# Top-k attention and two MLPs on one core: first value loads issued after key transposes, half of the second weights' low parts on GpSimd, later value norms at later steps

## The chip, the cores and the metric

One NeuronCore of a Trainium2 chip runs the whole program in one launch. The metric is the device time of an execution in microseconds. The kernel before took 1135.48 us (median of three runs, 1133.12 to 1138.31); the execution whose profile is shown here took 1133.29 us, of which the first to the last instruction span 1131.5 us. The engines are called as the profile calls them: PE (TensorE matmul) and PEld (its weight loads), DVE (VectorE), ACT (ScalarE), POOL (GpSimd), SP (SyncE, which only issues DMAs here). A queue of an engine runs in the order in which the program lists it: an instruction that waits holds everything behind it.

## The reference

Attention over 4 batches, 8 heads, 576 positions and head size 64, in which each row keeps only its 32 largest scores; then two MLPs on the 2304 tokens of width 512, with 2048 hidden units each.

```python
scores = (1/8) * q @ k.T                       # 4 x 8 x 576 x 576
kth = the 32nd largest of each row
attn = softmax(where(scores >= kth, scores, -1e9))
x = (attn @ v), heads side by side              # 2304 x 512
h = x @ w_in1;  g = where(h >= 1, h, where(h <= -1, 0, (h+1)**2/4));  y = g @ w_out1
out = relu(y @ w_in2)**2 @ w_out2
```

All inputs and the output are float32, and the result keeps float32-like accuracy by splitting each operand into a float16 high part and a float16 low part and adding three products.

## The kernel before

**Work.** The attention runs as 144 slots, one head of one tile of 128 query rows each (18 tiles T, 8 heads). A slot is: scores on PE into the PSUM tile `both`, which has room for two slots; eight DVE passes (four `max` for eight values each, `match_replace` between them) that find the 32nd largest score; `below` and `exp` on ACT into the tile `W`, for which POOL makes the bias `nb`; high part `pc` on ACT, low part on POOL; a DMA transpose of both parts (`pT`) on SP; the product with the values on PE (`acc`). After a tile's eight slots the tokens go through MLP 1 and then MLP 2, in 144 groups of 512 hidden units: in products (`h`), activation (`r`), split (`g`), a DMA transpose (`gT`), out products (`o`).

**Weights.** Four matrices of 16 chunks of 128x512 each (`i1`, `o1`, `i2`, `o2`) are loaded, decoded into a form of their own by ACT, POOL and DVE (`w_decode`, L475), squared into a Gram matrix on PE for a power-of-two scale (`w_norm`, L493), and split into high and low half (`w_split`, L519), where the two halves of a chunk overwrite the place of the chunk before it. For `i1` and `o1` the split is: high = scaled copy on ACT; low = two PE products into PSUM (a diagonal of the scale times the float32 chunk, less the high part: `lo_i`, `lo_o`), copied out by ACT. For `i2` and `o2`: scale in place (even chunks on ACT, odd ones on POOL), high = copy on ACT, low = subtraction on POOL.

**Values.** `v_load_early` (L619) brings the first batch's values in three DMAs of 512, 128 and 640 KB. For the batches 1 to 3, 24 pieces of the values are loaded and squared once more ahead of time for their scales (`norm_load`, `norm`, tile `n_v`); then `kv_scale`, `meet_consts`, `mlp1_consts` and `mlp2_consts` make scales and constants in small DVE instructions.

**Order.** Every instruction is recorded by `note` (L183) with the step u at which the table PLAN (L35) puts it; a slot has eight steps, so slot s begins at step 8s, and MLP group n stands 12 slots behind its slot number. `order` (L271) then lists the instructions of each engine: it plays the program with assumed costs (`costs`, L247), and of what is ready it takes the lowest step. The real program waits only on data; what `order` decides is each queue's sequence. Every instruction is emitted by one helper line, so all rows carry L348 (L356 after the change) and are told apart by their tiles. In the names, the number of a tile's buffer follows the name (`pT_339`), and rows of the profile leave it out; the program's weights, first keys and first values all live in one tile, `wall`.

The steps that the change touches: `v0l` is the step of `v_load_early`; `vn`, `vnd` and `vnl` set the first step, spacing and load lead of the 24 norms; `vs`, `meet`, `mc1` and `m2c1` the steps of the scales and constants.

Of the kernel before, what the change touches and what calls it, by code (L numbers as in the profile page):

```python
# [7 lines left out]
F16 = mybir.dt.float16  # L8
# [4 lines left out]
AF = mybir.ActivationFunctionType  # L13
# [24 lines left out]
    d0=(-8, -6, -4, -2), l0=(-9, -6), n0=(0, 1, 0, 1, 2, 3), q01=-5, v0l=-2, v0n=(5, 7, 9, 11), v0s=14, vn=60, vnd=7,  # L38
    vnl=18, vs=241, meet=248, mc1=252, m2c0=121, m2c1=265, v0=(21, 25, 29, 33, 37, 41, 45, 49), kv1=(254, 10, 289, 6),
# [10 lines left out]
    g_gate=13, g_split=15, scores=-6, below=8, wbufs=4, md=(), exp=9, bias=7, phi=10, plo=11, ptr=13, att=30, acopy=29, li1d=3, lo1=0, lo1d=0, dsd_i1=(), dsd_o1=(), dsd_i2=(), dsd_o2=(), xu0=2,  # L50
    dk=(0, 1, 2), dv=(8, 11, 5, 7), dq=(), dsh_i1=(), dsh_o1=(), dsh_i2=(), dsh_o2=(), odd=0, klead=10, vlead=5, sbufs=3,
    vbufs=8, dsa_i1=(0, 2, 4, 6, 8, 10, 12, 14), dsa_o1=(0, 2, 4, 6, 8, 10, 12, 14),
    dsa_i2=(0, 2, 4, 6, 8, 10, 12, 14), dsa_o2=(0, 2, 4, 6, 8, 10, 12, 14), u0=-6,
# [93 lines left out]
class Book:  # L147
# [3 lines left out]
    def __init__(self, nc):  # L151
        self.ops, self.rings, self.step, self.beat = [], {}, 0, []
        self.paper = _bacc_().Bacc("TRN2", target_bir_lowering=False, num_devices=1)
        self.names = 0
        self.shift = 0

# [26 lines left out]
    def note(self, engine, method, fn, args, kwargs):  # L183
# [7 lines left out]
        deps = set()  # L191
# [11 lines left out]
        for v in ins:  # L203
            c = v.cover()
            deps.update(n for d, n in v.tile.writes if meet(c, d))
            v.tile.reads.append((c, op.n))
# [40 lines left out]
    def costs(self, engine, method, args, kwargs, outs, ins):  # L247
        n = outs[0].elements() if outs else 0
        if engine == "PE":
            a = args[1].tile.dtype  # L250
            c = max(n * (4 if a is F32 else 1) / 2370.0, 0.03)
            return c, c + 0.2
        both = sum(not v.tile.ring.psum for v in ins if v.elements() > 64)
        if engine == "DVE":
            if method in ("max", "match_replace"):
                n = 576
            c = 0.06 + n / 960 + (0.07 if method == "match_replace" else 0.25 if both > 1 else 0.06 if method != "max" else 0)
            return c, c + 0.03
        if engine == "ACT":
# [101 lines left out]
def tile_topk_attention_mlp_mlp(  # L361
# [155 lines left out]
    DIAG_AT = {"i1": (38, 38), "o1": (48, 56)}  # L517

    def w_split(name, c):  # L519
# [3 lines left out]
        if name in DIAG_AT:  # L523

            diag = wall[:, DIAG_AT[name][c // 8], 0:P]
            ps = []

            def high():
                if c == 0 or c == 8 and len(set(DIAG_AT[name])) == 2:
                    DVE.tensor_scalar(diag, ident, s, None, op0=ALU.mult)  # L530
                ACT.activation(hi, src, AF.Copy, scale=s)

            def low():
                ps.append(ps_h.tile([P, 4, P], F32, tag="h", name=f"lo_{name}_{c}").rearrange("p a b -> p (a b)"))
                PE.matmul(ps[0], diag, src, start=True, stop=False)
                PE.matmul(ps[0], neg, hi, start=False, stop=True)

            return [high, low, lambda: ACT.activation(lo, ps[0], AF.Copy)]
        on_dve, one = c in PLAN["dsd_" + name], c in PLAN["dsh_" + name]
        if on_dve:  # L540
            scale = lambda: None
            low = lambda: DVE.scalar_tensor_tensor(lo, src, s, hi, op0=ALU.mult, op1=ALU.subtract)
            if one:
                high = lambda: DVE.tensor_scalar(hi, src, s, None, op0=ALU.mult)
            else:
                high = lambda: ACT.activation(hi, src, AF.Copy, scale=s)
        else:
            if c in PLAN["dsa_" + name]:
                scale = lambda: ACT.activation(src, src, AF.Copy, scale=s)
            else:  # L550
                scale = lambda: POOL.tensor_scalar(src, src, s, 1.0, op0=ALU.mult, op1=ALU.mult)
            low = lambda: POOL.tensor_tensor(lo, src, hi, op=ALU.subtract)
            if one:
                high = lambda: POOL.tensor_scalar(hi, src, 1.0, 1.0, op0=ALU.mult, op1=ALU.mult)
            else:
                high = lambda: ACT.activation(hi, src, AF.Copy)
        return [scale, high, low]
# [70 lines left out]
    kst, vst, ld = {}, {}, {}  # L628

    def k_prep(b, i):  # L630
# [26 lines left out]
        def trans():  # L657
            ks = pool.tile([P, 9, P], F16, tag="kst", name=f"kst_{b}_{i}", bufs=4)
            SP.dma_start_transpose(out=ks, in_=hl().rearrange("p c a d -> p (c a d)"))
            for h in range(2):  # L660
                kst[b, 2 * i + h] = ks[:, :, 64 * h : 64 * h + 64]
# [96 lines left out]
    def q_prep(T, half):  # L758
# [21 lines left out]
        def trans():  # L780
            qt = pool.tile([P, 2, 4, P], F16, tag="qT", name=f"qT_{T}_{half}", bufs=2)
            SP.dma_start_transpose(
# [69 lines left out]
    def prob_hi(t):  # L852
# [3 lines left out]
        ACT.activation(d["hi"], d["e"], AF.Copy)  # L856
# [38 lines left out]
    def token_trans(src, dst, key, tag, name):  # L895
# [9 lines left out]
        def trans():  # L905
            tt = pool.tile([P, 2, 4, P], F16, tag=tag, name=f"T_{name}", bufs=1)
# [101 lines left out]
    NGROUP = 8 * NTILE + 4  # L1008
# [21 lines left out]
    def mlp_act(n):  # L1030
# [8 lines left out]
        else:  # L1039
            ACT.activation(r, h, AF.Relu, scale=C2)  # L1040
            ACT.activation(r, r, AF.Square)
# [9 lines left out]
    def mlp_split(n):  # L1051
# [3 lines left out]
        ACT.activation(g[:, 0], r, AF.Copy)  # L1055
# [200 lines left out]
    order = [(1, 0, j) for j in range(4)] + ([(2, 0, j) for j in range(4)] if PLAN["early"] else [None] * 4)  # L1256
    order += [(1, 1, j) for j in range(4)] + ([None] * 4 if PLAN["early"] else [(2, 0, j) for j in range(4)])
    for T in range(2, NTILE):
        order += [(1, T, j) for j in range(4)] + [(2, T - 1, j) for j in range(4)]
    order += [(2, NTILE - 1, j) for j in range(4)]  # L1260
# [96 lines left out]
```

## Time and profile before

| what | value |
|---|---|
| median of three runs | 1135.48 us |
| the profiled execution | 1133.29 us, span 1131.5 us |
| busy: PE, DVE, ACT, POOL | 991.0, 917.4, 865.9, 702.0 us |
| slots start: 0, 4, 12, 16, 20 | 26.4, 50.9, 121.8, 157.4, 203.3 us |
| slots start: 36, 140 | 321.0, 997.8 us |

The slots' starts are those of their first `max` on DVE in the trace. From slot 36 to slot 140 a slot takes 6.5 us on average; the first twenty take 8.8 us each, while the weights are loaded, decoded and split beside the attention. DVE has little left after slot 143; PE then works off the last groups of the MLPs.

### The profile page before, as it was taken

Reading aid. Unit: us, or ns where it says so; the run is one execution under the profiler, and the core shown is the slowest. Engines: PE = TensorE matmul, PEld = TensorE weight load, DVE = VectorE, ACT = ScalarE, POOL = GpSimd, SP = SyncE. Lnnn points to the kernel's source line nnn. Section 1 sums busy time; section 2 is a strip of 40 time slices with the busy share of each in tenths; the row PEclk is TensorE's granted clock in tenths of the full one; section 3 lists DMA queues with packets and bytes.
Section 4 is the critical chain, followed back from the end, with each engine's and each line's share of the span. In section 5 each row is a group of like instructions: output and inputs, shape, how many; then the busy total and the mean of one; then the engine's idle time right before and its main releaser. Section 6 shows DMA issues by size and latency. Waiting matters only on the chain. (4 is left out here: it accounts for less than half of the span.)

```text
span 1131.5 us, 20715 instructions
## 1 busy us (share of the span) xinstructions
PE 991.0 (88%) x6700; PEld 483.0 (43%) x6700; DVE 917.4 (81%) x1967; ACT 865.9 (77%) x1613; POOL 702.0 (62%) x1166
## 2 busy tenths in 40 slices
PE   2257795778899989999999999999999999999997
PEld 1134342334344444444444444444544544444443
DVE  4899977897989898999989899998899999982100
ACT  4678999899777687878888777888777788776532
POOL 4696759879676755557776746567774647453221
PEclk9969898899999999999999999999999999999999
DMA  9988868575798666868977676778868665555332
GB/s 261 336 252 238 242 151 197 132 152 104 150 161 149 110 119 110 158 116 160 165 149 142 118 121 127 150 138 159 151 126 136 118 130 110 112 107 98 70 61 56
DMA packets 463389, 165.22 MB, mean 146 GB/s; under 512 B 441776, under 2 KB 448944, under 8 KB 463280
## 3 DMA queue, kind: packets, MB, share of 16 engines
q1 hardware_dynamic: 463280, 163.90, 71.0%
q8 instruction: 52, 0.85, 0.3%
q14 instruction: 57, 0.47, 0.1%
HBM read 55.31 MB, written 4.72 MB: 53 GB/s over the span
## 5 line engine op out<-in xcount | busy, mean ns | idle before, releaser
L348 PE MATMUL o<-wall,gT 128*128 128x512 f16 x1728 | 418.9, 381 | 17.5 <-DMA gT<-g 17.1
L348 DVE MAX8 m<-W 128x8 f32<-128x576 f32 x432 | 326.9, 758 | 8.5
L348 POOL TENSOR_TENSOR pc<-W,pc 128x64 f16<-128x64 f32 (+1 forms) x288 | 209.1, 747 | 87.8 <-ACT pc L348 73.2
L348 POOL TENSOR_TENSOR g<-r,g 128x512 f16<-128x512 f32 x144 | 167.7, 1164 | 152.4 <-ACT g L348 127.8
L348 PEld LDWEIGHTS <-gT 128*128 128x128 f16 x1728 | 163.7, 98 | 219.2 <-DMA gT<-g 31.6
L348 PE MATMUL h<-wall,T_x 128*128 128x512 f16 x864 | 209.4, 384 | 10.1 <-DVE r L348 8.3
L348 DVE MATCH_REPLACE8 W<-m,W 128x576 f32<-128x576 f32 x288 | 213.8, 743 | 0.0
L348 PE MATMUL h<-wall,T_y 128*128 128x512 f16 x864 | 207.9, 379 | 2.7 <-ACT r L348 1.7
L348 ACT ACTIVATE W<-both,nb 128x576 f32<-128x576 f32 x144 | 106.6, 740 | 91.7 <-DVE W L348 31.8
L348 DVE MAX8 m<-both 128x8 f32<-128x576 f32 x144 | 109.0, 757 | 44.0 <-PE both L348 23.4
L348 PE MATMUL both<-kst,qT 128*128 128x64 f16 (+3 forms) x640 | 101.7, 297 | 39.5 <-ACT W L348 28.6
L348 ACT ACTIVATE W<-W,nb,esc 128x576 f32<-128x576 f32 x144 | 124.1, 863 | 6.2 <-POOL nb L348 2.9
L348 PEld LDWEIGHTS <-T_x 128*128 128x128 f16 x864 | 82.1, 99 | 100.4 <-issue 13.1
L348 PEld LDWEIGHTS <-T_y 128*128 128x128 f16 x864 | 81.1, 98 | 93.2 <-issue 3.1
L348 PEld LDWEIGHTS <-pT 128*128 128x128 f16 (+1 forms) x2240 | 93.2, 102 | 52.4 <-issue 13.6
L348 ACT ACTIVATE g<-r 128x512 f16<-128x512 f32 x144 | 90.2, 627 | 30.3 <-DVE r L348 28.8
L348 PE MATMUL acc<-vst,pT 128*128 128x65 f16 (+1 forms) x2240 | 101.9, 197 | 7.8 <-ACT wall L348 3.9
L348 DVE MATCH_REPLACE8 W<-m,both 128x576 f32<-128x576 f32 x144 | 107.6, 747 | 0.0
L348 ACT ACTIVATE pc<-W 128x576 f16<-128x576 f32 x144 | 97.6, 678 | 0.9
L348 ACT ACTIVATE r<-r 128x512 f32<-128x512 f32 x144 | 90.3, 627 | 1.7
L348 POOL TENSOR_SCALAR nb<-m 128x1 f32<-128x1 f32 x144 | 30.5, 212 | 90.8 <-DVE m L348 78.1
L348 ACT ACTIVATE r<-h 128x512 f32<-128x512 f32 x72 | 42.6, 592 | 48.2 <-PE h L348 45.4
(143 smaller groups left out, 1127.9 us busy)
## 6 DMA issues: line engine op xcount, KB each, us to landing
wall<-in_moe_w_in_dram SPq DMA_DIRECT2D x32, 512.0 KB, 5.5
wall<-in_moe_w_out_dram SPq DMA_DIRECT2D x30, 512.0 KB, 5.5
out_dram<-ob SPq DMA_DIRECT2D x18, 256.0 KB, 2.5
l_q<-in_q_dram SPq DMA_DIRECT2D x16, 256.0 KB, 3.7
n_v<-in_v_dram SPq DMA_DIRECT2D x24, 144.0 KB, 3.1
n_k<-in_k_dram SPq DMA_DIRECT2D x12, 288.0 KB, 3.1
l_k<-in_k_dram SPq DMA_DIRECT2D x12, 288.0 KB, 3.3
pT<-pc SPq DMA_TRANSPOSE x144, 3.4
```

The source lines that it names most:

```text
L348: op.fn(*(real(a) for a in op.args), **{k: real(a) for k, a in op.kwargs.items()})
```

## The change

Three things are changed in PLAN and the functions it steers, and the order of all queues is made anew.

1. `v_load_early` moves from step -2 to step 0, and its three DMAs are listed only after the second key transpose (`hold`).
2. Of the 16 chunks of `o1`, the odd ones are split as the odd chunks of `i2` were: scale in place on POOL, copy on ACT, subtraction on POOL. The even ones stay as they were.
3. The 24 norms of the later values start at step 112 with a spacing of 6 (60 and 7 before), and the scales and constants that follow from them come 35 steps later.

Besides, `costs` assumes a smaller cost for one kind of DVE instruction. The new letters of `w_i1`, `w_i2` and `w_o2` and the other new entries stand for what was done before.

```diff
-    ... q01=-5, v0l=-2, v0n=(5, 7, 9, 11), v0s=14, vn=60, vnd=7,
-    vnl=18, vs=241, meet=248, mc1=252, m2c0=121, m2c1=265, ...
+    ... q01=-5, v0l=0, v0k=1, lag=1, tbufs=(1, 1), v0n=(5, 7, 9, 11), v0s=14, vn=112, vnd=6,
+    vnl=18, vs=276, meet=283, mc1=287, m2c0=121, m2c1=300, ...
+    w_i1="pppppppppppppppp", w_o1="pgpgpgpgpgpgpgpg", w_i2="agagagagagagagag", w_o2="agagagagagagagag",
@@ note
-        deps = set()
+        deps = set(self.hold)
@@ costs, DVE
+            if method == "tensor_scalar" and not any(v.tile.ring.psum for v in ins + outs):
+                n *= 0.8
@@ w_split
+        how = PLAN["w_" + name][c]
+        if how in "pP":
+            def low():
+                ps.append(ps_h.tile([P, 4, P], F32, tag="h", name=f"lo_{name}_{c}").rearrange("p a b -> p (a b)"))
+                PE.matmul(ps[1], ps[0], src, start=True, stop=False)
+                PE.matmul(ps[1], neg, hi, start=False, stop=True)
+            return [high, low, lambda: ACT.activation(lo, ps[1], AF.Copy)]
+        def scale():
+            if how == "a":
+                ACT.activation(src, src, AF.Copy, scale=s)
+            elif how == "g":
+                POOL.tensor_scalar(src, src, s, 1.0, op0=ALU.mult, op1=ALU.mult)
...
+        def high():
...
+                ACT.activation(hi, src, AF.Copy)
+        return [scale, high, lambda: POOL.tensor_tensor(lo, src, hi, op=ALU.subtract)]
@@ v_load_early
+        book.hold = turned[PLAN["v0k"] : PLAN["v0k"] + 1]
         SP.dma_start(t[0:64, :, 0:256], src[:, :, 0:256])
         SP.dma_start(t[0:64, :, 256:320], src[:, :, 512:576])
         SP.dma_start(t[64:128], src[:, :, 256:576])
+        book.hold = ()
@@ k_prep, trans
+            if b == 0:
+                turned.append(len(book.ops) - 1)
```

SP's queue at the start, before the change: `wall<-in_v_dram` are the three loads of the first values, `qT` and `kst` the transposes of the first queries and keys.

```order
L348 DMA wall<-in_moe_w_in_dram 128x1024 x6
L348 DMA wall<-in_v_dram 64x8x256
L348 DMA wall<-in_v_dram 64x8x64
L348 DMA wall<-in_v_dram 64x8x320
L348 DMA_TRANSPOSE qT_0_155<-qhl_0_125 128x8x128
L348 DMA_TRANSPOSE kst_0_166<-wall 128x9x128
L348 DMA_TRANSPOSE kst_1_181<-wall 128x9x128
L348 DMA_TRANSPOSE kst_2_190<-wall 128x9x128
L348 DMA_TRANSPOSE kst_3_200<-wall 128x9x128
L348 DMA_TRANSPOSE qT_1_218<-qhl_1_209 128x8x128
L348 DMA wall<-in_moe_w_in_dram 128x1024 x7
```

The same stretch after it:

```order
L356 DMA wall<-in_moe_w_in_dram 128x1024 x6
L356 DMA_TRANSPOSE qT_0_152<-qhl_0_122 128x8x128
L356 DMA_TRANSPOSE kst_0_163<-wall 128x9x128
L356 DMA_TRANSPOSE kst_1_178<-wall 128x9x128
L356 DMA_TRANSPOSE kst_2_187<-wall 128x9x128
L356 DMA_TRANSPOSE kst_3_199<-wall 128x9x128
L356 DMA_TRANSPOSE qT_1_215<-qhl_1_195 128x8x128
L356 DMA wall<-in_v_dram 64x8x256
L356 DMA wall<-in_v_dram 64x8x64
L356 DMA wall<-in_v_dram 64x8x320
L356 DMA wall<-in_moe_w_in_dram 128x1024 x7
```

The three value loads have moved past all six transposes of the first queries and keys, not past two alone; the weight loads on both sides stand where they stood.

ACT's queue, from the copies of the second half of the first queries on, before: `junk_v` are the norms of the first values, `W` with `both` is `below` of the slots 0 and 1, `W` with `esc` their `exp`.

```order
L348 ACTIVATE qhl_1_209<-qhl_1_209 128x4x64
L348 ACTIVATE junk_v_249,n_v<-wall 128x640
L348 ACTIVATE junk_v_255,n_v<-wall 128x640
L348 ACTIVATE wall<-wall 128x512
L348 ACTIVATE junk_v_263,n_v<-wall 128x640
L348 ACTIVATE wall<-wall 128x512
L348 ACTIVATE junk_v_273,n_v<-wall 128x640
L348 ACTIVATE W_229<-both,nb_271 128x576
```

And after:

```order
L356 ACTIVATE qhl_1_195<-qhl_1_195 128x4x64
L356 ACTIVATE W_227<-both,nb_259 128x576
L356 ACTIVATE W_231<-both,nb_266 128x576
L356 ACTIVATE W_227<-W_227,nb_259,esc_156 128x576
L356 ACTIVATE W_231<-W_231,nb_266,esc_156 128x576
L356 ACTIVATE pc_292<-W_227 128x576
L356 ACTIVATE junk_v_297,n_v<-wall 128x640
L356 ACTIVATE pc_302<-W_231 128x576
```

The norms of the first values, which need the moved loads, now stand behind the first two slots' `below` and `exp`.

POOL's queue around slot 11, before: `nb` is a slot's bias, `pc` the low part of its probabilities, `wall<-wall` of TENSOR_SCALAR a step of the decode.

```order
L348 TENSOR_SCALAR wall<-wall 128x512
L348 TENSOR_TENSOR pc_1135<-W_984,pc_1135 128x64
L348 TENSOR_TENSOR pc_1135<-W_984,pc_1135 128x512
L348 TENSOR_SCALAR nb_1180<-m_11_1068 128x1
L348 TENSOR_SCALAR wall<-wall 128x512
L348 TENSOR_SCALAR nb_1180<-m_11_1068,esc_482 128x1
```

After:

```order
L356 TENSOR_SCALAR wall<-wall,s_o_1114 128x512
L356 TENSOR_TENSOR pc_1129<-W_961,pc_1129 128x64
L356 TENSOR_TENSOR pc_1129<-W_961,pc_1129 128x512
L356 TENSOR_SCALAR wall<-wall,s_o_1114 128x512
L356 TENSOR_SCALAR nb_1167<-m_11_1055 128x1
L356 TENSOR_SCALAR wall<-wall 128x512
L356 TENSOR_SCALAR nb_1167<-m_11_1055,esc_509 128x1
L356 TENSOR_SCALAR wall<-wall,s_o_1114 128x512
L356 TENSOR_SCALAR wall<-wall 128x512
L356 TENSOR_TENSOR wall<-wall 128x512
```

The scalings of odd `o1` chunks (`wall<-wall,s_o`) and their subtractions (TENSOR_TENSOR `wall<-wall`) now stand among the attention's own instructions, eight of each from slot 10 to slot 16.

## Rows read from the trace of the kernel before

**Rows 1.** The page, parts 1 and 2: busy us, and DVE's forty slices.

```profile
PE 991.0 (88%) x6700; PEld 483.0 (43%) x6700; DVE 917.4 (81%) x1967; ACT 865.9 (77%) x1613; POOL 702.0 (62%) x1166
DVE  4899977897989898999989899998899999982100
```

**Rows 2.** Windows: stretch, length, busy of PE, PEld, DVE, ACT, POOL; clock, DMA, GB/s.

```profile
26.40:60.00 33.60, 7.69 (x50) 4.11 (x50) 30.12 (x67) 21.12 (x41) 21.11 (x36) 1.00 1.05 336
60.00:120.00 60.00, 41.70 (x305) 23.09 (x303) 56.18 (x128) 49.79 (x98) 47.52 (x75) 0.83 0.87 233
120.00:200.00 80.00, 60.71 (x370) 28.91 (x367) 66.36 (x129) 75.31 (x148) 58.43 (x75) 0.89 0.77 196
200.00:260.00 60.00, 45.13 (x299) 21.82 (x297) 52.67 (x117) 53.15 (x115) 49.57 (x74) 0.89 0.66 136
260.00:300.00 40.00, 32.36 (x217) 15.14 (x214) 35.74 (x96) 34.24 (x66) 33.15 (x48) 1.00 0.64 121
300.00:1020.00 720.00, 695.42 (x4925) 340.55 (x4924) 654.97 (x1386) 568.76 (x1034) 450.32 (x804) 1.00 0.73 134
1020.00:1131.50 111.50, 102.18 (x517) 46.31 (x515) 11.84 (x27) 49.88 (x87) 28.83 (x33) 1.00 0.37 70
```

**Rows 3.** Timeline of SP, 0 to 60 us: start, length, queue, line, operation.

```profile
3.26 3.48 SPq L348 DMA_DIRECT2D wall<-in_moe_w_in_dram  x6
7.02 5.11 SPq L348 DMA_DIRECT2D wall<-in_v_dram  x3
12.26 6.19 SPq L348 DMA_TRANSPOSE qT<-qhl  x1
```

**Rows 4.** DMA issues at 6.3 and 12.3 us: KB, us from issue to landing.

```profile
wall<-in_moe_w_in_dram SPq DMA_DIRECT2D x1, 512.0 KB, 10.2
...
qT<-qhl SPq DMA_TRANSPOSE x1, 11.1
```

**Rows 5.** Timeline of POOL, PE and DVE, 20 to 41 us, with idle before.

```profile
20.50 0.64 POOL L348 TENSOR_SCALAR wall<-wall 128x512 int32<-128x512 uint16 x1
...
21.17 0.69 DVE L348 SCALAR_TENSOR_TENSOR wall<-wall 128x512 int32<-128x512 int32 x1 [1.89 <-POOL wall L348]
...
24.32 2.08 PE L348 MATMUL both<-kst,qT 128*128 128x64 f16 x8 [1.78 <-DMA kst<-wall]
...
26.43 0.77 DVE L348 MAX8 m<-both 128x8 f32<-128x576 f32 x1 [4.56 <-PE both L348]
...
36.11 1.28 DVE L348 SCALAR_TENSOR_TENSOR wall<-wall 128x512 int32<-128x512 int32 x2
...
40.12 0.77 DVE L348 MAX8 m<-both 128x8 f32<-128x576 f32 x1 [2.38 <-PE both L348]
```

**Rows 6.** Tile `lo_o`: shortest, median, longest ns; first and last start, us.

```profile
L348 PE MATMUL lo_o<-wall x32: 592/592/1202, 122.6 to 166.4; 128*128 128x512 f32 x32
L348 PE MATMUL lo_o<-wall,neg x16: 376/379/379, 123.5 to 166.8; 128*128 128x512 f16 x16
L348 ACT ACTIVATE wall<-lo_o x16: 582/597/642, 124.6 to 167.5; 128x512 f16<-128x512 f32 x16
```

**Rows 7.** Tile `wall` on POOL and DVE, the same columns.

```profile
L348 POOL TENSOR_TENSOR wall<-wall x32: 1146/1159/1611, 171.4 to 280.4; 128x512 f16<-128x512 f32 x32
...
L348 POOL TENSOR_SCALAR wall<-wall,s_i x8: 687/692/697, 167.1 to 206.7; 128x512 f32<-128x512 f32 x8
...
L348 DVE SCALAR_TENSOR_TENSOR wall<-wall x26: 668/693/1580, 120.4 to 204.0; 128x512 int32<-128x512 int32 x26
```

**Rows 8.** Tile `n_v`, the same columns.

```profile
L348 ACT ACTIVATE n_v<-n_v x24: 426/433/466, 76.7 to 266.0; 128x288 f32<-128x288 f32 x24
L348 ACT ACTIVATION_READ_ACCUMULATOR n_v<-n_v x24: 186/192/224, 77.1 to 266.3; 128x1 f32 x24
```

**Rows 9.** DVE's groups, 262 to 303 us: count, busy us, mean ns, idle before.

```profile
L348 DVE TENSOR_SCALAR mc<-mc 128x5 int32<-128x5 int32 (+1 forms) x3 | 2.1, 701 | 0.0
...
L348 DVE TENSOR_REDUCE gsm_v<-n_v 128x1 f32<-128x8 f32 x1 | 0.1, 141 | 0.0
```

More of the change, by code (lines that the diff above doesn't have):

```diff
@@ L49 @@
     ych=(0, 1, 2, 3, 5, 6, 10, 10, 73), yu=36, ou=28, z0=200, g_in=(9, 9, 9, 9), g_out=(20, 22, 23, 26), g_act=11,
[L50 to L53, printed above, removed]
+    g_gate=13, g_split=15, scores=-6, below=8, wbufs=4, md=(), exp=9, bias=7, phi=10, plo=11, ptr=13, att=30, acopy=29, li1d=3, lo1=0, lo1d=0, xu0=2,
+    dk=(0, 1, 2), dv=(8, 11, 5, 7), dq=(), odd=0, klead=10, vlead=5, sbufs=3,
+    vbufs=8,
+    w_i1="pppppppppppppppp", w_o1="pgpgpgpgpgpgpgpg", w_i2="agagagagagagagag", w_o2="agagagagagagagag",
+    phd=(), ghd=(), sq=(), u0=-6,
     prio=(3, 0, 0, 2, 2, 3, 4, 5, 5, 6, 1, 7), gbufs=2, g_tr=18,
@@ L155, in __init__ @@
         self.shift = 0
+        self.hold = ()
     def tile(self, pool, bufs, shape, dtype, tag, name, given, psum):
@@ L204, in note @@
             c = v.cover()
-            deps.update(n for d, n in v.tile.writes if meet(c, d))
+            before = [n for d, n in v.tile.writes if meet(c, d)]
+            assert before, (method, v.tile.name)
+            deps.update(before)
             v.tile.reads.append((c, op.n))
@@ L517, in tile_topk_attention_mlp_mlp, with w_diag @@
     DIAG_AT = {"i1": (38, 38), "o1": (48, 56)}
+    diags = {}
+    def w_diag(name, half):
+        at = DIAG_AT[name][half]
+        if (name, at) not in diags:
+            diags[name, at] = wall[:, at, 0:P]
+            DVE.tensor_scalar(diags[name, at], ident, W[name]["s"], None, op0=ALU.mult)
+        return diags[name, at]
     def w_split(name, c):
@@ L522, in w_split @@
         s = W[name]["s"]
[L523 to L526 removed]
+        how = PLAN["w_" + name][c]
+        ps = []
+        if how in "pPdD":
             def high():
[L529 to L531 removed]
+                if how in "pP":
+                    ps.append(w_diag(name, c // 8))
+                if how in "PD":
+                    DVE.tensor_scalar(hi, src, s, None, op0=ALU.mult)
+                else:
+                    ACT.activation(hi, src, AF.Copy, scale=s)
@@ L533, in low @@
+        if how in "dD":
+            return [lambda: None, high, lambda: DVE.scalar_tensor_tensor(lo, src, s, hi, op0=ALU.mult, op1=ALU.subtract)]
+        if how in "pP":
             def low():
                 ps.append(ps_h.tile([P, 4, P], F32, tag="h", name=f"lo_{name}_{c}").rearrange("p a b -> p (a b)"))
-                PE.matmul(ps[0], diag, src, start=True, stop=False)
-                PE.matmul(ps[0], neg, hi, start=False, stop=True)
-            return [high, low, lambda: ACT.activation(lo, ps[0], AF.Copy)]
@@ L539, in w_split @@
[L539 to L544, printed above, removed]
-            else:
[L546 to L549, printed above, removed]
-            else:
[L551 to L556, printed above, removed]
@@ L557, in w_split @@
-        return [scale, high, low]
+                PE.matmul(ps[1], ps[0], src, start=True, stop=False)
[6 more added lines that the diff above has]
+                POOL.tensor_scalar(src, src, s, 1.0, op0=ALU.mult, op1=ALU.mult)
+            else:
+                DVE.tensor_scalar(src, src, s, None, op0=ALU.mult)
@@ L855, in prob_hi @@
         d["hi"] = d["pc"][:, 64 : 64 + S] if t % 2 else d["pc"][:, 0:S]
-        ACT.activation(d["hi"], d["e"], AF.Copy)
+        if t in PLAN["phd"]:
+            DVE.tensor_scalar(d["hi"], d["e"], 1.0, None, op0=ALU.mult)
+        else:
+            ACT.activation(d["hi"], d["e"], AF.Copy)
     def prob_lo(t):
@@ L1040, in mlp_act @@
             ACT.activation(r, h, AF.Relu, scale=C2)
-            ACT.activation(r, r, AF.Square)
+            if T in PLAN["sq"]:
+                DVE.scalar_tensor_tensor(r, h, C2, r, op0=ALU.mult, op1=ALU.mult)
+            else:
+                ACT.activation(r, r, AF.Square)
     def mlp_gate(n):
@@ L1255, in tile_topk_attention_mlp_mlp @@
     N0 = PLAN["N0"]
[L1256 to L1260, printed above, removed]
+    lag = PLAN["lag"]
+    order = []
+    for T in range(lag):
+        order += [(1, T, j) for j in range(4)] + [None] * 4
+    for T in range(lag, NTILE + lag):
+        order += [(1, T, j) for j in range(4) if T < NTILE] + [(2, T - lag, j) for j in range(4)]
     assert len(order) == NGROUP
```

23 lines of the change are left out of this document (15 added, 8 removed).

## The prediction

> **What bounds the kernel now.** I read the page first: PE is the busiest engine with 991 of 1131.5 us, DVE comes next with 917, and DVE's slices fall to 2 and less at the end, so that the span closes with PE's own tail [rows 1]. An average over the span does not say which engine sets the pace where the change acts, so the windows come next [rows 2]. From 300 to 1020 us PE is busy 695.4 of 720 us (96.6%, at full clock): that stretch is PE's, DVE has 9% to spare, and PE alone works in the 111 us behind it. Before 300 us PE is nowhere full. From 26 to 120 us DVE is (86.3 of 93.6 us); from 120 to 200 us ACT is the fullest with 75.3 of 80, beside POOL with 58.4 and DVE with 66.4; from 260 to 300 us DVE has 35.7 of 40 and PE 32.4. All three edits act before about 330 us. Slots and MLP groups stand interleaved in the lists, and from about slot 100 on the lists are nearly what they were. So I count what each edit does to the time at which the PE-bound stretch begins, and carry that 1:1 to the end.
>
> **The first values' loads.** SP finishes issuing the six weight loads at 6.7 us, spends 5.1 us on the three value loads, and starts the first query transpose at 12.3 us [rows 3]. The last weight load lands at 6.3 + 10.2 = 16.5 us, the query transpose at 12.3 + 11.1 = 23.4 us [rows 4]: transfers land in the order of the queue, and the 1.28 MB of values lie between. Without them the query transpose lands about 6 us sooner, and so could the first scores, which start at 24.32 [rows 5]. DVE can't take all of it: the slot's first `max`, at 26.43, stands in its list behind a decode step that ends at 21.17 + 0.69 = 21.86 and waits for POOL's at 20.50, neither of which needs values or queries. The idle time before that `max` is 4.56 us, and that is the most the edit can give. Part is paid back at once: behind the first two slots DVE now has two decode steps of 1.28 us together in the wait for slot 2's scores, from 36.11 to 40.12 [rows 5]; in the new list slot 2's `max` follows directly, so the wait stays empty and the 1.3 us are done later. Net 4.6 - 1.3 = 3.3 us; the bounds are 4.6 and 0.
>
> The 0 stands for a cover that may be missing. The held loads now follow six transposes, and their norms on ACT stand behind the first two slots' `below`, `exp` and one `pc`; that is beside slot 2's first `max`, at 40.1 - 4.6 = 35.5 us. The loads land, by my estimate, at about 31 us: the second query transpose at 25, somewhat behind the landing of the first today, then the same 6 us of transfer. So the norms find them there. The weight loads behind them land about when they do now: what leaves the queue ahead of the transposes comes back behind them. If the norms are late instead, ACT's list stands still with decode steps and `below` of slot 2 behind it, and DVE loses what it gained.
>
> **The second weights' low parts.** Eight chunks lose, on PE, two float32 products of 0.592 us and one of 0.379 each, so 8 x 1.563 = 12.5 us; on ACT eight copies of 0.597, so 4.8 us [rows 6]. They gain, on POOL, eight scalings (0.692) and eight subtractions (1.159), read from the same work on the third weights: 8 x 1.851 = 14.8 us [rows 7]. ACT's high half stays, as a copy without scale. The place is 122 to 168 us.
>
> PE is not full there (60.7 of 80, at a mean clock of 0.89 [rows 2]), so PE's 12.5 us shorten nothing by themselves. ACT's 4.8 us do: 70.5 us of ACT work at the share it reaches now (94%) take 75 us, 5 less than 80. Against that POOL rises from 58.4 to 73.2 us, 98% of those 75. So the gain is at most 5.0 us; at worst POOL keeps all the idle time it has now (21.6 us, spent in waiting for others) and the stretch becomes 58.4 + 14.8 + 21.6 = 94.8 us long, a loss of 14.8. I take a gain of 3: ACT is the one that is full now, and POOL would fit, though barely. There is a second path: an odd chunk's subtraction must have read its place before the next chunk's high half overwrites it, so the split of sixteen chunks passes eight times through POOL's list, behind `nb` and `pc` of slots 11 to 16.
>
> On this the Trainium skill speaks against the change: SBUF — State Buffer, section "Who interferes with whom", says that a VectorE instruction with two SBUF inputs and a GpSimd instruction that reads SBUF exclude each other for a whole instruction. The decode step on DVE is of that kind: 26 of them between 120 and 204 us take 0.668 at least, 0.693 in the middle and 1.580 at most [rows 7], so holds of up to 0.9 us are seen, though rarely. With POOL busy 18% more of the time (14.8 of 80) and half of 0.9 us per hold, 26 x 0.18 x 0.45 = 2.1 us are lost, and the sum would be 2.1 us higher.
>
> **The later values' norms.** 24 squares of 0.433 us and as many reads of the sum of 0.192 us lie between 76.7 and 266.0 us [rows 8]. They now lie from slot 14 (about 140 us) to slot 31 (about 287 us). Some eight leave the stretch to 140 us and come back after 200; inside 120 to 200 us ACT has nine or ten of them before and eight or nine after, so I put no gain on ACT. Their 24 loads move with them, off SP's list at 67 to 140 us, where SP issues in time anyway: nothing. What counts is behind them. The scales, `meets`, `mc` and their like are 21 groups of small DVE instructions between 262 and 303 us, from 2.1 us down to 0.1 [rows 9], and add up to 9.8 us in a stretch where DVE is the fuller engine. They move 35 steps on, some 30 us, into the PE-bound stretch, where DVE's spare 9% of 40 us hides 3.6 us of them. Bounds: 0, and 7.6 us, which is all of PE's idle time from 260 to 300 us. I take 2, nearer to the 3.6 that can be hidden.
>
> **Sum.** 3.3 + 3 + 2 = 8.3 us less, from 1133.3 us of the profiled execution to 1125.0. The profiled execution is 2.2 us under the median of the runs shown, so as a median 1127.
>
> **Rivals.**
>
> *Given back.* Only one of the parts survives: DVE starts earlier but then waits for weights and `pT`, which stand behind the same bytes in the DMA queue as before (DMA share 1.05 to 60 us, 0.87 to 120 us [rows 2]), or PE's stretch finds its own new gaps in lists made anew. For it: the DMA engines are full to 60 us. Against it: DVE is busy 94% from 60 to 120 us, so it waits little there. Gain 3 us: 1130.3, as a median 1132.5.
>
> *POOL becomes the bound, slower.* The handovers through POOL's list hold the split, and ACT and PE wait for it; decode, `nb` and `pc` of the slots stand behind the new instructions. For it: POOL would be at 98%, and `nb` releases `below`, which releases the scores of the next slot but one. Against it: the subtractions are off the attention's own path, and POOL's idle time is waiting that can be moved. It decides once the stretch grows by more than 9.0 us, the 5.7 that count as slower and the 3.3 of the start, that is once less than 5.8 of POOL's 21.6 idle microseconds can be used. At full price: 1133.3 + 14.8 - 3.3 = 1144.8, as a median 1147.
>
> *DVE and POOL exclude each other*, by the rule above, as holds like the one of 1.580 us: 2.1 us of the gain go, 1127.1, as a median 1129.3.
>
> That the change does not do what it says holds in one point only: the loads wait for six transposes, not for two, which gives the whole of what the queue can give.
>
> **Numbers.** What a measurement of this kernel can tell from no change is 0.5%, 5.7 us: faster is below 1129.8, slower above 1141.2. Forecast 0.60, with a range of its own of 1118 (all upper bounds: 4.6 + 5.0 + 7.6 = 17.2 us less) to 1132; 0.53 of it faster, 0.07 same. Given back 0.22: 0.04 faster, 0.18 same. POOL 0.14: 0.11 slower, 0.03 same. Exclusion 0.04: half faster, half same. Together 0.59 faster, 0.30 same, 0.11 slower. The range for 8 in 10 runs from 1117 to 1140: it takes in all but the worst of the second rival.
>
> **What would show it.** The first `max` near 21.9 us instead of 26.4; the first values landing near 31 us and no wait of ACT for them; ACT less than 75 us busy in the same sixteen-chunk stretch, POOL near 73, and slot 20 starting 5 to 7 us sooner than at 203.3 us; DVE's constants at 300 to 340 us with PE full beside them; slot 36 some 8 us before 321.0, and the same distance at slot 140. It is wrong if slot 12 gains less than 2 us, if POOL's subtractions are what ACT or PE wait for in that stretch, or if a lead at slot 36 is gone at slot 140.

## The result: 1.1% slower

The changed kernel took 1149.84 us (median of four runs, 1148.00 to 1151.55) against 1136.89 for the kernel before on the same chip: a ratio of 1.0107, 95% interval 1.0086 to 1.0127. Measured again later, beside the last experiments, it was 1.0123 (1.0106 to 1.0140). The forecast was 1127 us, a gain of 0.7%.

**The profile after.** The page answers [rows 1]: PE and ACT are less busy than before, POOL is busier by 16 us, DVE by 4, and the span is 15.4 us longer. The busy times hardly differ, so the time was lost to waiting and, as shown below, to PE work at half its clock.

```profile
PE 986.7 (86%) x6676; PEld 478.1 (42%) x6676; DVE 921.5 (80%) x1967; ACT 862.2 (75%) x1605; POOL 718.3 (63%) x1182
```

The windows, with the columns of [rows 2]:

```profile
120.00:200.00 80.00, 52.56 (x367) 25.43 (x365) 65.99 (x133) 70.88 (x138) 74.60 (x91) 0.94 0.79 197
...
300.00:1020.00 720.00, 687.00 (x4827) 334.96 (x4827) 653.51 (x1391) 560.34 (x1023) 444.80 (x791) 0.99 0.73 133
```

In the stage of the second weights ACT came down to 70.9 us and POOL up to 74.6, nearly as worked out (70.5 and 73.2). But the PE-bound stretch, which the forecast had taken as given, has PE busy 687.0 us instead of 695.4 [rows 2], and its mean clock is 0.99 instead of 1.00: it opens gaps of its own.

Where the time goes is seen best in the starts of the slots (first `max`), here as us against before, from one profiled execution each. The same kernel twice (second and third row) differs by up to 5.5 us at single slots, and the profiled execution of before lies 2 to 5 us under the medians of before. So a difference of less than some 6 us in one row says little by itself, and the ratios decide; a smaller step counts only where several rows share it and a wait in the trace stands behind it.

| slot | 0 | 4 | 12 | 20 | 36 | 44 | 72 | 76 | 100 | 140 |
|---|---|---|---|---|---|---|---|---|---|---|
| before, us | 26.4 | 50.9 | 121.8 | 203.3 | 320.9 | 377.3 | 558.5 | 584.4 | 737.4 | 997.7 |
| after | -1.8 | -0.8 | -0.1 | +0.6 | +3.2 | +8.8 | +6.5 | +14.3 | +13.5 | +16.7 |
| after, again | -1.6 | -0.6 | +2.1 | +6.1 | +8.0 | +12.3 | +8.9 | +17.0 | +16.2 | +18.4 |
| n1_cost | -0.5 | -0.5 | -1.0 | +0.9 | +0.9 | +1.0 | -3.0 | +3.9 | +3.1 | +3.9 |
| s_hold | -1.6 | -0.6 | +2.6 | +5.8 | +13.1 | +17.4 | +15.6 | +19.7 | +24.3 | +27.0 |
| s_gps | +0.1 | 0 | 0 | -4.2 | +3.7 | 0 | +0.9 | +8.1 | +7.4 | +8.4 |
| s_norms | +0.1 | +0.1 | +1.3 | +2.8 | +7.8 | +16.2 | +16.8 | +21.0 | +26.3 | +27.5 |
| pin_a | -1.4 | +0.2 | +0.3 | +0.4 | 0 | +0.1 | +2.0 | +2.0 | +2.1 | +3.6 |
| pin_a2 | -4.9 | +0.1 | +1.5 | +2.0 | +2.0 | +2.2 | +2.6 | +2.6 | +3.2 | +4.0 |
| pin_b | 0 | 0 | +0.1 | +1.8 | +1.7 | +1.9 | +1.2 | +1.3 | +4.6 | +5.7 |
| pin_c | 0 | 0 | -0.3 | -0.5 | +1.2 | +4.8 | +6.2 | +6.2 | +6.7 | +9.6 |
| pin_c2 | +0.8 | +0.8 | +0.8 | +1.1 | -1.2 | +2.2 | +3.2 | +3.2 | +3.4 | +4.9 |
| pin_abc | -2.0 | -0.2 | -0.4 | +0.4 | +2.7 | +6.4 | +4.1 | +4.2 | +9.3 | +9.2 |
| pin_y6b | -1.7 | -0.8 | +2.0 | +5.5 | +7.6 | +11.8 | +8.5 | +12.5 | +13.1 | +15.1 |
| pin_n1 | +0.3 | +0.3 | -0.2 | +1.9 | +3.4 | +4.3 | +0.9 | +5.1 | +6.8 | +7.7 |

The start of the changed kernel is 1.8 us sooner (3.4 at slot 2), and that is gone at slot 8 (+0.9). From slot 12 to slot 20 the two executions lose 0.7 and 4.0 us; from slot 20 to 48 another 9 and 6; and both lose 8 in one place, slots 72 to 76. The longest waits there, on DVE and PE (idle time and its releaser in brackets):

```profile
586.69 0.77 DVE L356 MAX8 m<-both 128x8 f32<-128x576 f32 x1 [2.96 <-PE both L356]
...
598.64 0.77 DVE L356 MAX8 m<-both 128x8 f32<-128x576 f32 x1 [5.39 <-ACT W L356]
```

```profile
578.35 0.52 PE L356 MATMUL acc<-vst,pT 128*128 128x65 f16 x6 [3.58 <-DMA pT<-pc]
578.67 7.42 PE L356 MATMUL o<-wall,gT 128*128 128x512 f16 x24
585.93 0.65 PE L356 MATMUL both<-kst,qT 128*128 128x64 f16 x4
```

None of the three edits touches anything at 570 us. What stands there has only been listed in another order.

A gap on PE can cost more here than its own length. The prediction has PE at full clock in this stretch, and in the kernel before the granted clock is 1.00 from 300 to 1020 us [rows 2]. In the changed kernel it is 0.50, the lower of TensorE's two levels (1.2 and 2.4 GHz), in three places behind a gap. Windows of the same form as above:

```profile
351.00:354.00 3.00, 3.00 (x27) 1.55 (x25) 2.81 (x7) 2.70 (x5) 2.14 (x3) 0.50 0.78 74
406.00:408.60 2.60, 2.60 (x8) 0.96 (x8) 1.34 (x3) 2.60 (x5) 0.15 (x1) 0.50 0.61 113
578.60:582.80 4.20, 4.20 (x15) 1.58 (x13) 4.17 (x9) 3.87 (x6) 2.56 (x9) 0.50 1.00 220
```

PE had stood idle for 3.49, 3.26 and 3.58 us just before or at the start of these windows. Behind the last gap the first ten of the 24 `o` products follow each other at 0.43 us, the rest at 0.21, so that the scores of the next slot come some 2 us later still. PE works 9.8 us in the three windows; at full clock that would be 4.9, so by this estimate some 5 us of the 13.5 that are lost between slots 36 and 140 are lost clock.

### The profile page after: what moved, and what is told of

It reads as the page before. It is cut to its first block, busy times and chain, and to the rows that moved or that the text cites. A ratio compares the mean times of both kernels' runs of the same rounds, so it can differ in the third digit from the quotient of the medians.

```text
span 1146.9 us, 20673 instructions
## 1 busy us (share of the span) xinstructions
PE 986.7 (86%) x6676; PEld 478.1 (42%) x6676; DVE 921.5 (80%) x1967; ACT 862.2 (75%) x1605; POOL 718.3 (63%) x1182
## 5 line engine op out<-in xcount | busy, mean ns | idle before, releaser
L356 PE MATMUL o<-wall,gT 128*128 128x512 f16 x1728 | 420.2, 383 | 19.0 <-DMA gT<-g 16.6
L356 PE MATMUL h<-wall,T_x 128*128 128x512 f16 x864 | 213.2, 390 | 10.2 <-DVE r L356 6.6
L356 DVE MAX8 m<-both 128x8 f32<-128x576 f32 x144 | 109.0, 758 | 52.8 <-PE both L356 27.5
```

Of the source, the lines that this page charges most:

```text
L356: op.fn(*(real(a) for a in op.args), **{k: real(a) for k, a in op.kwargs.items()})
```

## The experiments

Two theories. *Lists*: the time is lost because all queues were listed anew, by a planner whose assumed times are not the chip's, and not by what the edits do (that the assumed times are the reason is not tested here). *Edits*: one of them costs by itself; the texts call this POOL, held loads or norms.

### Each part alone, lists made anew

The base is the kernel before, whose order these runs keep if nothing is edited. n1_cost takes only the planner's lower assumed cost, no instruction changes:

```diff
+            if method == "tensor_scalar" and not any(v.tile.ring.psum for v in ins + outs):
+                n *= 0.8
```

> The kernel before with one thing of the change alone: the smaller assumed cost of one kind of DVE instruction, which adds, removes and re-times no instruction and only makes the lists anew. Theory 'lists' (the 12 us come from how the lists of all engines fell when they were made anew, not from any of the three edits): the time moves by 3 us or more from before, either way. Theories 'POOL' (the low parts on GpSimd cost the 12 us) and 'held loads' (the later value loads cost them): within 2 us of before.

s_hold takes only the held loads:

```diff
-v0l=-2
+v0l=0, v0k=1
+        book.hold = turned[PLAN["v0k"] : PLAN["v0k"] + 1]
```

> The kernel before with the held value loads alone. 'Held loads': 8 to 15 us slower, as the full change. 'POOL': 0 to 4 us faster, as in the prediction's first term. 'Lists': any sign, and no relation to the first max on DVE, which should start about 2 us earlier, as in the full change.

s_gps takes only the odd `o1` chunks:

```diff
-w_o1="pppppppppppppppp"
+w_o1="pgpgpgpgpgpgpgpg"
```

> The kernel before with the odd chunks of the second weights split on GpSimd alone. 'POOL': 8 to 15 us slower, with the loss complete by slot 24 (some 235 us), POOL over 18 of 20 us busy between 120 and 200 us. 'Lists': slots 16 and 20 within 2 us of before, as in the full change, and whatever is lost or won comes later, in waits of PE or DVE behind something else in their lists.

s_norms takes only the later norms, scales and constants:

```diff
-vn=60, vnd=7, ... vs=241, meet=248, mc1=252, ... m2c1=265
+vn=112, vnd=6, ... vs=276, meet=283, mc1=287, ... m2c1=300
```

> The kernel before with the later norms, scales and constants alone. By the prediction's third term 2 us faster (0 to 7.6). 'Lists': any sign, several us, and the three single edits with the cost's change don't add up to the 12 us of the whole.

Measured, as a ratio to before: n1_cost 1.0026 (1.0008 to 1.0044), s_hold 1.0228 (1.0195 to 1.0261), s_gps 1.0053 (1.0033 to 1.0074), s_norms 1.0216 (1.0187 to 1.0246). The parts alone cost 3 + 26 + 6 + 25 = 60 us, the whole 12 to 14. Costs of edits would add up; these don't. And the lists made anew lose time with no edit at all: 3 us, as little as *lists* allowed. For s_hold and s_norms *lists* allowed any sign, so these two speak against costs of the edits rather than for *lists*; s_gps missed one point of it, as slot 20 came 4.2 us sooner instead of within 2. In the table s_hold and s_norms lose some 7 us behind slot 76, hundreds of microseconds after what they change, and n1_cost and s_gps have the changed kernel's loss at slots 72 to 76.

### The edits inside the old lists

The decisive runs take the lists of before and put only the edited instructions elsewhere in them, by their planned start time; everything else stays in its row (in the traces the engines' rows are those of before outside the stretch that each edit moves):

```diff
-        book.emit(book.order())
+        book.emit(pin(book.order(), book, nc, "A", odd))
```

pin_a: the three value loads moved to the second query transpose. In the trace the first of them is issued just ahead of it, at 22.31 us against 23.39, and two behind it; so it is for pin_a2 and pin_abc, too.

```diff
+        if "A" in PINS and op.move == "dma_start" and step == -2:
+            t = 24.021 + 0.001 * (op.n % 3)
```

> Only the three loads of the first values are moved, inside the kernel before's own lists: on SP from behind the first weight loads to just behind the second query transposition; every other instruction on every engine stays where it stood. 'Lists' theory (the loss of the changed kernel comes from all lists being made anew, not from its edits): the first max comes 2 to 4.5 us sooner than 26.4 us and the time is 0 to 3 us below before, nothing like the +26 us of the same edit with lists made anew. 'Held loads' theory (holding the loads back costs by itself, because the norms of the values and the weights behind them come late): 5 us or more above before, and the offset is there by slot 12.

pin_b: at each odd `o1` chunk the ACT copy and the two kinds of PE products go, POOL's scaling and subtraction come.

```diff
+            if kind in ("mm1", "mm2", "copy"):
+                continue
+                (SCALE_AT[c], nc.gpsimd, "tensor_scalar", (src, src, s, 1.0), dict(op0=ALU.mult, op1=ALU.mult)),
+                (SUB_AT[c], nc.gpsimd, "tensor_tensor", (lo, src, hi), dict(op=ALU.subtract)),
```

> Only the odd chunks of the second weights go to GpSimd, inside the before's own lists: at each of the eight places the ACT copy and both PE matmuls go, a GpSimd scale and a GpSimd subtract are put into GpSimd's idle stretches. 'Lists': between -3 and +1 us against before, where the same edit with lists made anew gave +6. 'POOL' theory (GpSimd work in this stage costs by itself): +4 us or more, and the offset appears between slots 12 and 20.

pin_c: norms and constants at their later places.

```diff
+                t = later[k] if op.engine == "ACT" else later[k - 2] + 0.01 if k > 1 else later[0] - 16 + 5 * k
+                t += when(264) - when(229)
```

> Only the later values' norms with their loads, and the scales and constants made from them, move to their later places (norms by 52 to 29 steps, the rest by 35), inside the before's own lists. 'Lists': between -3 and +2 us, where the same edit with lists made anew gave +25. 'Norms cost by themselves': +5 us or more, appearing between slots 30 and 45, where the constants stand now.

pin_abc: all three.

> All three edits inside the before's own lists. 'Lists': the terms of the prediction should then come through as far as their sizes are right: between -8 and 0 us against before. 'Edits' (the three cost what the changed kernel lost): +8 to +15 us as the changed kernel.

Measured: pin_a 0.9998 (0.9982 to 1.0013), pin_b 1.0015 (1.0000 to 1.0030), pin_c 1.0042 (1.0022 to 1.0061), pin_abc 1.0047 (1.0030 to 1.0065). So the held loads cost nothing where they cost 26 us with new lists, and the odd chunks cost 0 to 3 us; here the parts add up within the intervals (0 + 2 + 5 against 5). But no edit gains either. pin_abc missed both theories: *lists* expected 0 to -8 us, *edits* +8 to +15. pin_b and pin_c, too, lie between what the two theories had expected of them. Of the changed kernel's 12 to 14 us some 5 are there with the old lists; the other 7 to 9, by difference, come with the new ones.

pin_c's loss turned out to be partly my placing. On ACT the norms had come to stand close, with a wait for a load among them; a slot's `below` stood behind them, and DVE waited at slot 26:

```profile
245.78 0.44 ACT L356 ACTIVATE n_v<-n_v 128x288 f32<-128x288 f32 x1 [1.33 <-DMA n_v<-in_v_dram]
...
248.27 0.77 DVE L356 MAX8 m<-both 128x8 f32<-128x576 f32 x1 [4.58 <-PE both L356]
```

pin_c2 spaces them evenly:

```diff
-            later[k] = max(when(112 + 6 * k) + op.start - when(60 + 7 * k), later.get(k - 1, 0) + 0.8)
+            later[k] = when(112 + 6 * k)
```

> The later norms, scales and constants moved inside the before's lists as in the run that gave +4.8 us, but the 24 norms now spaced evenly by six steps. In that run seven norms had come to stand within 12 us of ScalarE's list around 234 to 247 us, one waiting 1.3 us for its load, and a slot's mask behind them came 3.4 us late. 'Placement' theory: the +4.2 us at slot 26 is gone and the end is -1 to +3 us against before. 'Norms cost by themselves': still +4 us or more.

1.0026 (1.0006 to 1.0045), and that wait is 0.60 us. So at its better place the part costs some 3 us where I had a gain of 2; the two placings by hand differ by 2 us, within the intervals. In the table pin_c, pin_c2 and pin_abc all lose 3.4 to 3.7 us between slots 36 and 44, where the constants now stand on DVE. In pin_c2 DVE is busy 54.9 us between these two starts, before 50.3, and PE stands idle 4.9 us instead of 1.7; its longest wait there is for DVE's `x`, 0.69 us before:

```profile
349.04 0.95 PE L356 MATMUL acc<-vst,pT 128*64 128x65 f16 x28 [2.02 <-DVE x L356]
```

The changed kernel has the same wait at 350.55 us, of 3.49 us; behind it stands the first of the three stretches at half clock.

### Where the first lead went

In pin_a the queue does what was worked out: the query transpose is issued at 12.3 us and lands at 17.4. But the first `max` comes at 25.01 only, and the lead of 1.4 us is gone at slot 2:

```profile
22.45 0.61 PE L356 MATMUL gram_i<-wall 128*128 128x128 bf16 x4 [1.98 <-DVE wall L356]
...
32.91 0.74 ACT L356 ACTIVATE junk_v<-wall 128x640 bf16<-128x640 f32 x1 [9.54 <-DMA wall<-in_v_dram]
```

PE's list has four `gram` products ahead of the first scores, and they wait for the very decode step that I had called unrelated to the queries. On ACT the norms of the first values wait 9.5 us for their loads with `below` behind them. pin_a2 moves both out of the way:

```diff
+            if names[0].startswith("junk_v_") and op.engine == "ACT":
+                t = (37.95, 38.55, 39.1, 39.7)[int(one[7:])]
+            elif op.engine == "PE" and one == "gram_i1" and step == 3:
+                t = 24.62 + 0.001 * (op.n % 8)
```

(the scale from the norms, the first values' splits and two decode steps follow them).

> As the run that moved only the first value loads inside the before's lists (first max 1.4 us sooner, the lead gone at slot 2, time unchanged), and now what stood in the way is moved too, by hand and only in the first 50 us: on TensorE the last 4 gram matmuls behind the first scores, on ScalarE the four norms of the first values and two decodes behind the first two slots' masks and exponentials, with the scale made from the norms 4.6 us later. 'The lead was eaten by the places in the lists': first max near 23, slot 2 some 2 to 4 us sooner than 40.1, and 1 to 4 us below the before at the end if such a lead carries 1:1 as I had it. 'The decode stage takes it anyway' (slots 4 to 12 are bound by the weights' decoding on VectorE, ScalarE and GpSimd, which gets no shorter): slot 2 is sooner, slot 12 is within 1 us of 121.8, and the end within 2 us of before.

1.0026 (1.0007 to 1.0045): no gain, but 3 us over before, nearer to the second expectation than to the first. The first `max` now comes 4.9 us sooner, the full bound, and DVE finds no work behind it:

```profile
21.54 1.43 DVE L356 MAX8 m<-both 128x8 f32<-128x576 f32 x2
...
38.45 0.77 DVE L356 MAX8 m<-both 128x8 f32<-128x576 f32 x1 [7.15 <-PE both L356]
```

```profile
34.32 0.64 POOL L356 TENSOR_SCALAR wall<-wall 128x512 int32<-128x512 uint16 x1 [0.61 <-POOL wall L356]
35.04 0.34 POOL L356 TENSOR_SCALAR nb<-m 128x1 f32<-128x1 f32 x2
```

```profile
35.26 1.37 ACT L356 ACTIVATE W<-both,nb 128x576 f32<-128x576 f32 x2 [12.79 <-POOL nb L356]
```

The idle time before slot 2 has grown from 2.38 us [rows 5] to 7.15: the two slots' `nb` stand in POOL's list behind two decode steps, the second of which starts at 34.32 us on weights that landed at 34.19, no sooner than they did (33.82 in the kernel before). So the list order ties slot 2 to the weights here. It need not: in the changed kernel `nb` stands ahead of these decode steps, and slot 2 starts 3.4 us sooner than before. There the lead is gone at slot 8: from slot 2 to slot 8 DVE runs 19 decode steps in 16.6 us, where it ran 17 in 13.3, and has 1.6 us more of waits. `nb` ahead of the decode steps inside the old lists was not tried.

### What in the new lists costs

In the changed kernel I followed the waits at 578 to 599 us to one buffer. The half-precision splits of queries, of x and of y and the scratch of the squares share a single one, in turn. Before the change, ACT's rows for it:

```profile
552.51 0.41 ACT L348 ACTIVATE qhl<-qhl 128x256 f16<-128x256 f16 x1
...
559.71 0.69 ACT L348 ACTIVATE hl_y<-o,sy 128x512 f16<-128x512 f32 x1 [0.39 <-DMA qT<-qhl]
```

After it:

```profile
572.47 0.40 ACT L356 ACTIVATE qhl<-qhl 128x256 f16<-128x256 f16 x1
...
577.90 0.68 ACT L356 ACTIVATE hl_y<-o,sy 128x512 f16<-128x512 f32 x1
...
583.76 0.63 ACT L356 ACTIVATE junk_q<-l_q 128x512 bf16<-128x512 f32 x1 [1.11 <-DMA T_y<-hl_y]
```

POOL's part of this split is done at about 564.5 us, but the copy `qhl<-qhl` stands 8 us further down ACT's list. Before the change it stood 2 us further down. So `hl_y` of tile 6 starts 18 us after the split of the queries (559.79 us) instead of 12 after it (547.33). I took this to free the PSUM bank late for tile 7's `o` products. The trace does not bear that out: PE runs dry at 574.8 and waits for `pT` of the product listed ahead of them, and the `o` products start at 578.67, ahead of DVE's part of `hl_y` (579.29 to 580.03). What the rows show is the order in PE's list: 24 `o` products in one piece, behind a late `pT` and ahead of the scores. Next in line for the buffer is the square of tile 10's queries; its scale is late, and POOL waits for it with slot 75's `nb` further down its list, at 596.32 us:

```profile
591.03 0.69 POOL L356 TENSOR_SCALAR l_q<-l_q,sq 128x512 f32<-128x512 f32 x1 [3.06 <-DVE sq L356]
```

pin_y6 is the changed kernel with its own lists, of which it moves that chain and the 24 `o` products:

```diff
+    to = {("ACT", "activation", 573, "qhl_9_1"): 514.6, ("SP", "dma_start_transpose", 574, "qT_9_1"): 515.3,
+          ("ACT", "activation", 546, "hl_y6"): 519.7, ("DVE", "scalar_tensor_tensor", 550, "hl_y6"): 520.6,
+          ("SP", "dma_start_transpose", 550, "T_y6"): 521.8}
+    for u in (564, 566, 567, 570, 572, 574, 575, 578):
+        to["PE", "matmul", u, "o_1_7"] = 522.6 if u < 572 else 525.5
```

> The changed kernel with its own lists, and 29 of its 11500 instructions put up to 8 us sooner in them: the copy of the low part of the query half 9_1 (ScalarE) right behind GpSimd's subtract, its transposition, then the split and transposition of the second MLP's input of tile 6 that wait for the same single buffer, and the 24 matmuls of tile 7's first MLP that wait for the PSUM bank this split frees. 'One buffer held' theory of the loss at slots 74 to 76: that loss (+8 us) shrinks to under +3, and the time is 4 to 8 us below the changed kernel, a ratio of about 1.004 to 1.007 to before. If the loss there has another cause: within 2 us of the changed kernel, 1.009 or more.

1.0083 (1.0057 to 1.0110): not distinguishable from the changed kernel by itself, less than expected. The first wait (2.96 us) was gone, the second (5.4 us) not, although the square now starts at 580.59 us without waiting for the buffer. So the buffer does not make the second wait; of the first, the run moved the buffer's chain and the `o` products together and can't say which of them it was. a_oldcost is the whole change planned with the old assumed DVE cost (n1_cost's diff taken back):

> The whole change except the lower assumed cost of VectorE's SBUF-to-SBUF operations in the planner: the same instructions as the changed kernel, in lists made with the old assumption. 'Lists' theory: the time moves by several us for no instruction at all; anything from 1136 to 1165, and not within 1 us of the changed kernel's. 'Edits' theory: within 2 us of the changed kernel, since the instructions are the same.

1.0077 (1.0048 to 1.0106), 1145.34 us: by the ratios 3 to 5 us under the changed kernel for the same instructions, at the edge of the intervals; it speaks for *lists* without proving it. pin_y6b adds to pin_y6 that slot 76's scores stand ahead of the `o` and `h` products, and the split of the next queries behind slot 75's mask; after_again is the changed kernel itself, for comparison on that chip:

```diff
+    to["PE", 594, "both"] = 539.1
+    to["ACT", 595, "r_61"], to["ACT", 619, "qhl_10_0"] = 546.0, 546.6
```

> The changed kernel's lists with the same 29 instructions sooner as before (chain of the one buffer and tile 7's 24 matmuls), and now also what then ended the second wait (VectorE's 5.5 us before slot 76's first max): the four matmuls of that slot's scores are put ahead of 24 MLP matmuls in TensorE's list, and on ScalarE the split of query half 10_0, which waited 3.1 us for the same buffer, stands behind slot 75's mask and exponential instead of ahead of them. 'The places in the lists around slots 72 to 76 cost 8 us': the wait at slot 76 falls below 2 us, slots 76 to 140 lie 5 to 8 us sooner than in the changed kernel, and the time is 4 to 8 us below it. 'It is only put off': the wait moves to the slots behind, and the time is within 2 us of the run before this.

> The changed kernel itself once more, beside the two runs that move single rows of its lists, so that they are compared on the same chip. Ratio to before 1.0086 to 1.0127 as first measured.

1.0071 (1.0058 to 1.0084) against 1.0123 (1.0106 to 1.0140): 5.2 us faster (1146.54 against 1151.77) by moving 36 of 11500 instructions by some microseconds. This shows that places in the list cost time in the changed kernel, with no instruction added or removed. In the profiles 4.5 us of it are there at slot 76 and 3.3 at slot 140, less than the 5 to 8 expected. PE's long gap there is gone, and the clock is 1.00 from 575 to 586 us. The waits on DVE are now

```profile
596.91 0.77 DVE L356 MAX8 m<-both 128x8 f32<-128x576 f32 x1 [4.08 <-ACT W L356]
```

so the second did not fall below 2 us as I had expected: POOL's `nb` still stands behind the late scale there. That last link was read, not tried. pin_n1 makes the same moves in n1_cost:

> The kernel before's instructions in the lists that the other assumed VectorE cost alone gives (measured +3 us; 3 us ahead of before at slot 72 and 4 behind at slot 76, with the changed kernel's wait row for row), with the same rows moved at slots 70 to 76. If these places are what it lost: 2 to 7 us below that kernel, so between -4 and +1 us against before, a version that may beat both kernels. If it is only put off: +3 us as without.

1.0006 (0.9991 to 1.0020), 2 us less than without. That the same rows cost time in lists that no edit has touched is not shown: the intervals overlap (1.0008 to 1.0044 without), and in the profile slots 72 to 76 still lose 4.2 us, of 6.9. No run beat the kernel before.

## Why the prediction was wrong

**The steps that failed** are two, and the larger is the sum itself: -8.3 us of terms, of which each was to shorten the way to the PE-bound stretch. Inside the old lists, where nothing else moves, they measure +5.3 (pin_abc); that is 13.6 of the 21 us by which the forecast missed. The other is the premise that each edit's effect on the beginning of the PE-bound stretch is carried 1:1 to the end, PE running there "at full clock" as before. By difference lists made anew cost 7 to 9 us more.

Where they cost it, the starts of the slots show. From slot 100 on the lists are nearly the same, as I had them (of DVE's 565 rows there 19 stand elsewhere, the last near slot 129), and the offset grows by some 3 us. But between slots 36 and 100 it grows by 10 (+3.2 to +13.5): in the wait for the constants, which is the third edit's, in the gaps at 406 and 578 us, which no edit explains, and in the half clock behind them. I had named this among the rivals as "PE's stretch finds its own new gaps in lists made anew", but only as a way to lose part of the gain; the rival that ended slower was another. That matmuls at half clock can follow a gap on PE is in no term and no rival. Each of the six orders that the planner made after a disturbance is slower than the order of before, by 3 to 26 us beyond what the edits cost inside the old lists, the 3 of them at the edge of the intervals. Why the order of before is so much better was not tested.

**The first values, -3.3 us.** The bound of 4.6 was right (4.9 with the way cleared), and so was the transfer. Two things were missed. The `gram` products stand on PE between the decode step and the scores, so the first `max` came at 24.6 and not at 21.9. And beyond them the lead is not kept: in pin_a2 slots 0 and 1 wait for POOL's decoding of weights that land no sooner, and the idle time before slot 2 grows by what slot 0 gains; in the changed kernel slot 2 leads by 3.4 us, and DVE pays most of it back to slot 8 in decode steps. The two that I had seen put off were priced at 1.3 us; from slot 2 to slot 8 these steps take 3.3 us more. Measured, 0 us, the lower bound.

**The second weights, -3 us.** The sizes were right (ACT 70.9 of 80, POOL 74.6), the conclusion was not: that the stretch shrinks to what keeps ACT at 94%. ACT now has 9 us of idle time in it, and slot 20 starts 0.6 and 6.1 us later in the two executions, not 5 to 7 sooner. ACT was the fullest engine there, but few of DVE's waits between 120 and 200 us ended with its work: in the kernel before, the `gram` products on PE ended 4.5 us of them, POOL's decode 2.6, ACT some 2. In the old lists the part costs 0 to 3 us. *POOL becomes the bound*, at +14.8, did not happen either, with POOL 93% busy. As to the exclusion of DVE and POOL in SBUF — State Buffer of the Trainium skill, section "Who interferes with whom": the trace agrees that the one waits until the other has ended. The four longest decode steps of 120 to 204 us in the kernel before each end 0.54 or 0.55 us after a POOL instruction that had begun before them. The price goes by the order: the mean of these steps is 0.82 us in the kernel before, 0.78 in the changed kernel, 0.85 in pin_b and 0.99 in s_gps, so between nothing and 26 x 0.17 = 4.4 us, with 2.1 estimated; slot 20 came no later for it in s_gps.

**The later norms, -2 us.** The sign was wrong: +5 as first placed, +3 when spaced evenly. DVE's work on them is the same in both places: the 39 small instructions take 10.5 us before and 10.7 in pin_c2. What was mis-sized is the part that PE's stretch hides, 3.6 us by DVE's spare 9%. Between slots 36 and 44 DVE gets 4.6 us more to do and the slots take 3.4 us longer, since PE waits for what DVE makes behind the constants.

**Sum.** -8.3 us were forecast and +12 to +14 measured: +5 from the edits as they were placed in the old lists, 7 to 9 from lists made anew.

## What to carry to other kernels

Where a planner orders the queues, a change of one step is a new order of everything it reaches, and the price of that can be several times that of the edit: forecast it as a term of its own, with its spread taken from lists made anew without an edit. To judge an edit, put it by hand into the old order first; what it gains or costs there is its own, and that of the place it got. The engine that is fullest in a stage is not the one to relieve unless the waits say that the others wait for it. And where PE is the bound, read the granted clock behind each of its gaps: what follows at half clock is part of the price.

## What the hardware showed unexpectedly

The same small DVE instructions took very different times in different places: the `mc` group 161 ns (pin_c2), 467 ns (after) and 701 ns (before) on average, and one 128x2 `tensor_tensor` on `sv` 1174 ns in pin_c2. The traces show why. Of the 39 scales and constants in each of the executions of before, after and pin_c2, 21 in the three together took over 0.4 us, and every one of these ended 0.02 to 0.05 us after a POOL instruction that had begun before it:

```profile
327.17 1.17 DVE L356 TENSOR_TENSOR sv<-sv 128x2 f32<-128x2 f32 x1
```

```profile
327.06 1.28 POOL L356 TENSOR_TENSOR khl<-l_k,khl 128x576 f16<-128x576 f32 x1
```

Others that ran beside POOL's work were not held. One that is held costs DVE what is left of POOL's instruction, and another order only hands the wait to another one: 161 ns for `mc` in pin_c2 came with 1174 for `sv` and 1008 for `NG`. POOL's scaling of a chunk, 0.69 us in the middle, took up to 1.64 in the changed kernel's second stage. And the first query transpose landed 5.1 us after its issue with only weight loads ahead of it, where it took 11.1 with the value loads between [rows 4].
